# Expert weight conversion paced behind the dense layer's pieces, and half of g's low parts on GpSimd

## The chip, the cores and the metric

One core of one Trainium2 chip. The metric is the device time of one execution in microseconds (us), lower is better; each kernel is run several times.

## What is computed

Three layers follow each other (numpy, cut to what matters):

```python
def _attn_ref(q, k, v, g_norm):                  # q, k, v: 8 x 8 x 576 x 64
    kv = np.einsum('bhsd,bhse->bhde', k, v)
    out = np.einsum('bhsd,bhde->bhse', q, kv)
    rms = np.sqrt(np.mean(out * out, axis=-1, keepdims=True) + 1e-06)
    return out / rms * g_norm

def _moe_ref(x, w_in, w_out, alpha):             # x: 4608 x 512, w_in: 512 x 2048
    h = x @ w_in
    g = np.maximum(h, 0.0) + alpha * np.minimum(h, 0.0)
    return g @ w_out

def _moe2_ref(x, w_gate, w_output_gate, w1, w2): # 8 experts, w1[e]: 512 x 1024
    logits = x @ w_gate
    e_idx = np.argmax(logits, axis=1)
    ...
    for e in range(E):
        mask = e_idx == e
        out[mask] = gate_w[mask, None] * eom[mask, e, None] * (np.maximum(x[mask] @ w1[e], 0.0) @ w2[e])
```

## The kernel before, in words

Every float32 operand of a large product is split into two float16 halves, a high part and what is left (low part), and a product is three float16 matmuls: high by high, high by low, low by high. The 4608 tokens are 12 blocks of 384 (NBLK = 12), each of three tiles of 128.

The first 205 us are a stage whose order is written out by hand (`plan`, under `manual_schedule`): weights of the dense layer, attention for blocks 0 to 2, and the dense layer for blocks 0 and 1. Then come blocks 2 to 11, in which the order of each engine's queue is made by a list scheduler: it takes the instructions in the order in which the program writes them as their rank, and puts on each engine the first one that its own timing model holds to be ready. `tc.issue_after(ins)` adds the rule that what is written inside stands behind `ins` in the queue of the same engine. After block 11 come the expert slots, whose order on TensorE is again by hand.

A block i of 2 to 11 is written as `emit_h_block(i)`, then `emit_y_block(i)`.

- `emit_h_block` has 16 pieces f of h (128 of 2048 columns). A piece is 12 matmuls of 384 columns (`h_sum`, L689), ScalarE's scaled copy m out of PSUM (`h_copy`, L694), VectorE's maximum r (`h_bend`, L703), ScalarE's cast of r to the high part of g (`h_split`, L708) and VectorE's subtraction that makes the low part of g (L709). m and r have two buffers each, PSUM has two banks for h (`ps_h`). In the first stage GpSimd makes the low part (`start` is true), in blocks 2 to 11 VectorE does.
- `emit_y_block` has three row groups u of 128 tokens. Each is 48 matmuls of 512 columns (`y_products`, L724), three for each f, in two banks (`ps_y`). What is ready first goes first, so row groups of y are interleaved with pieces of h. The result is copied out (ysb, L736), scaled and split into rows (`y_tail`), turned by a transposing DMA, and goes to the logits (L802), the routing (`route_1`, `route_2`) and a scatter to DRAM by GpSimd (L868).
- After each piece, and after every fifth f of y, `tick` runs one item of each of several lists: `yq` (logits, routing), `side` (scatters), `attq` and, as often as it is told, `exq`.
- `attq` holds `att_steps(i)`, the attention for block i, 14 steps for i = 3 and on: q scaled on GpSimd (L328), split and transposed, products on TensorE (ops, L350), squares on ScalarE (L359), sums and scales on VectorE (L369 to L400), the power on GpSimd (L376), the cast (L411), the low part on GpSimd (L416) and the transposing DMA that makes x (L422). `att_steps(3)` runs in block 2's h pieces, `att_steps(i + 2)` from the y part of block i on.
- `exq` holds `expert_jobs`: 16 matrices of the experts (w1 and w2 of 8), each in four pieces of 128 x 1024. A piece is loaded (rawe, five buffers), its magnitude taken on ScalarE (eab, L624) and gathered on VectorE (L627). Then the maximum over partitions follows: a transpose on TensorE (allmax, L150), a row maximum on VectorE (L152), a matmul that spreads it (L154), in the one bank of `ps_l`, which logits and ranks use too. Then each piece is split into halves (ScalarE L475, VectorE L476) and stored to `ws`. Before, a matrix is 8 steps; `emit_h_block` runs a step at every third piece (6 per block), `emit_y_block` 9 per block. All of it must be done when block 10 ends.

Of the kernel before, what the change touches and what calls it, by code (L numbers as in the profile page):

```python
# [10 lines left out]
F32 = mybir.dt.float32  # L11
F16 = mybir.dt.float16
BF16 = mybir.dt.bfloat16
# [53 lines left out]
def body(ctx: ExitStack, tc, q, k, v, g_norm, w_in, w_out, alpha, w_gate, w_og, w1, w2, out):  # L67
# [76 lines left out]
            dve.tensor_scalar(out=out_s.bitcast(I32), in0=out_inv.bitcast(I32), scalar1=-1.0, scalar2=float(254 << 23),  # L144
                              op0=ALU.mult, op1=ALU.add)

    def all_max(am, nm):
        n = am.shape[1]
        ps = ps_l.tile([P, P + E], F32, tag="l", name="allmax" + nm)
        pe.transpose(ps[:n, 0:P], am, ident)  # L150
        m = small.tile([E, 1], F32, tag="amrow", name="amrow" + nm)
        dve.tensor_reduce(out=m[:n], in_=ps[:n, 0:P], axis=AX.X, op=ALU.max)  # L152
        if n == 1:
            pe.matmul(ps[:, P:P + 1], ones32[:1, :], m[:1], start=True, stop=True)  # L154
            return ps[:, P:P + 1]
        d = small.tile([E, E], F32, tag="amdiag", name="amdiag" + nm)
        dve.tensor_scalar(out=d[:n, :n], in0=ident[:n, :n], scalar1=m[:n], scalar2=None, op0=ALU.mult)
        pe.matmul(ps[:, P:P + n], ones32[:n, :], d[:n, :n], start=True, stop=True)
        return ps[:, P:P + n]
# [314 lines left out]
    def split(dst_h, dst_l, src, s):  # L474
        act.activation(out=dst_h, in_=src, func=AF.Copy, scale=s)  # L475
        dve.scalar_tensor_tensor(out=dst_l, in0=src, scalar=s, in1=dst_h, op0=ALU.mult, op1=ALU.subtract)  # L476

    def finish_max(am, nm):
        m = small.tile([P, 1], F32, tag="amx", name="amx" + nm)
        dve.tensor_reduce(out=m, in_=am, axis=AX.X, op=ALU.max)  # L480
        return all_max(m, nm)

    class Dense:

# [119 lines left out]
    def expert_jobs():  # L604
        raws = {}

        def load(n):
            if n < 8 * E:
                m, i = divmod(n, 4)
                src = (w1, w2)[m % 2][m // 2]  # L610
                r = src.shape[0] // 4
                t = rawp.tile([P, 1024], F32, tag="raw", name=f"rawe_{n}")
                sp.dma_start(out=t.rearrange("p (c f) -> p c f", f=src.shape[1]),
                             in_=src[i * r:(i + 1) * r, :].rearrange("(c p) f -> p c f", p=P))
                raws[n] = t

        for n in range(4):
            load(n)
        for m in range(2 * E):
            nm = f"_w{m}"  # L620
            am = cv.tile([P, 512], BF16, tag="acc", name="eam" + nm, bufs=1)
            for i in range(4):
                ab = cv.tile([P, 2, 512], BF16, tag="c", name=f"eab{nm}_{i}", bufs=3)
                act.activation(out=ab.rearrange("p a b -> p (a b)"), in_=raws[4 * m + i], func=AF.Abs)  # L624
                for h in range(2):
                    if i or h:
                        dve.tensor_tensor(out=am, in0=am if i else ab[:, 0, :], in1=ab[:, h, :], op=ALU.max)  # L627
                if i == 0:
                    load(4 * m + 4)
                yield  # L630
            for w in (256,):
                dve.tensor_tensor(out=am[:, 0:w], in0=am[:, 0:w], in1=am[:, w:2 * w], op=ALU.max)
            r = finish_max(am[:, 0:256], nm)
            s = small.tile([P, 1], F32, tag="es", name="es" + nm)
            inv = small.tile([P, 1], F32, tag=f"ei{m % 2}", name="ei" + nm)
            pow2(r, nm, s, inv)
            for i in range(4):
                w = ws[m // 2, :, m % 2 * 8192:(m % 2 + 1) * 8192].rearrange("p (t c) -> p t c", t=2)
                hi = stg.tile([P, 1024], F16, tag="hl", name=f"whi{nm}_{i}")
                lo = cv.tile([P, 1024], F16, tag="am", name=f"wlo{nm}_{i}")  # L640
                split(hi, lo, raws[4 * m + i], s)
                for t, (eng, x) in enumerate(((act, hi), (sp, lo))):
                    eng.dma_start(out=w[:, t, i * 1024:(i + 1) * 1024], in_=x)
                if i < 3:
                    load(4 * m + 5 + i)
                yield
            if m % 2 == 0:
                inv1 = inv
            else:
                dve.scalar_tensor_tensor(out=kexp[:, m // 2:m // 2 + 1], in0=inv1, scalar=1.0 / CB, in1=inv,  # L650
                                         op0=ALU.mult, op1=ALU.mult)


    attq, yq, exq, side = [], [], [], []

    def step(gens):
        while gens:
            if next(gens[0], "end") != "end":
                return
            gens.pop(0)  # L660
# [5 lines left out]
    def tick(n_expert=0):  # L666
        if yq:
            yq.pop(0)()
        if side:
            side.pop(0)()  # L670
        step(attq)
        for _ in range(n_expert):
            step(exq)


    def h_piece(i, f, g, start):
# [7 lines left out]
    def h_sum(i, f, ps):  # L684
        fs = slice(f % 4 * P, (f % 4 + 1) * P)
        n = 0
        for c in range(NC):
            for w, xc in ((0, c), (0, NC + c), (1, c)):
                pe.matmul(ps, wi[:, f // 4 * NC + c, w, fs], xt[i][:, xc, :], start=(n == 0), stop=(n == 3 * NC - 1))  # L689
                n += 1  # L690

    def h_copy(i, f, start, ps):
        r0 = tp.tile([P, BLK], F32, tag="m", name=f"m_{i}_{f}")
        act.activation(out=r0, in_=ps, func=AF.Copy, scale=(scst if start else scal)[:, f:f + 1])  # L694
        return i, r0

    def h_unit(f, g, start, part):
# [2 lines left out]
    def h_bend(f, part):  # L700
        i, r0 = part
        r = tp.tile([P, BLK], F32, tag="r", name=f"r_{i}_{f}")
        dve.scalar_tensor_tensor(out=r, in0=r0, scalar=alphat[:, f:f + 1], in1=r0, op0=ALU.mult, op1=ALU.max)  # L703
        return r

    def h_split(f, g, start, r):
        hi, lo = g[:, 0, f % GF, :], g[:, 1, f % GF, :]
        act.copy(out=hi, in_=r)  # L708
        (pool if start else dve).tensor_tensor(out=lo, in0=r, in1=hi, op=ALU.subtract)  # L709

    def emit_h_block(i):
        for f in range(NF):
            h_piece(i, f, gts[f // GF], False)
            if i == 2:
                for todo in (yq, side):
                    if todo:
                        todo.pop(0)()
            tick(f % 3 == 0)
        xt.pop(i)

    def y_products(ps, g, f, u, start, stop, **kw):
        us = slice(u * P, (u + 1) * P)
        for m, (t, w) in enumerate(((0, 0), (0, 1), (1, 0))):
            pe.matmul(ps, g[:, t, f % GF, us], wo[:, f, w, :], start=(start and m == 0), stop=(stop and m == 2), **kw)  # L724

    def emit_y_block(i):
        b = y_state(i)
        for u in range(TB):
            ps = ps_y.tile([P, DM], F32, tag="y", name=f"y_{i}_{u}")
            for f in range(NF):  # L730
                y_products(ps, gts[f // GF], f, u, f == 0, f == NF - 1)
                if f % 5 == 4:
                    tick(1)
            if i < NBLK - 1:
                ysb = cv.tile([P, DM], F32, tag="c", name=f"ysb_{i}_{u}", bufs=3)
                act.copy(out=ysb, in_=ps)  # L736
                ps = ysb
            y_tail(i, u, ps, *b)
        yq.append(lambda: route_1(i, *b))
# [43 lines left out]
    def row_turned(i, u, lg, rows, wait):  # L783
        nm = f"_{i}_{u}"
        rowt = rowts[u]
        row = rowt[:, 0:DM].bitcast(F16)
        rows.append(rowt)
        yT = tp.tile([P, 2 * NC, P], F16, tag="yT", name="yT" + nm, bufs=2)
        t = sp.dma_start_transpose(out=yT, in_=row)
        if (i, u) == (NBLK - 1, 0):  # L790
            sp_last[0] = t.ins
            rows_ahead()

        def logits():
            lps = ps_l.tile([P, 32], F32, tag="l", name="l" + nm)
            for c in range(NC):
                mm = [(yT[:, c, :], wg16[:, c].rearrange("p a b -> p (a b)"), lps),
                      (yT[:, NC + c, :], wg16[:, c, 0, :], lps[:, 0:16])]
                if c == NC - 1:
                    mm.reverse()  # L800
                for x, (a, w, o) in enumerate(mm):
                    pe.matmul(o, a, w, start=(c == 0 and x == 0), stop=(c == NC - 1 and x == 1))  # L802
            dve.tensor_reduce(out=lg[:, u, :], in_=lps.rearrange("p (t c) -> p c t", t=2), axis=AX.X, op=ALU.add)

        yq.extend([lambda: None] * wait + [logits])
# [720 lines left out]
```

## Time and profile before

| | us |
|---|---|
| median of three runs | 1359.05 |
| the three runs | 1351.5, 1359.05, 1364.7 |
| the profiled execution | 1348.63 |
| its span, first to last instruction | 1346.9 |
| mean granted TensorE clock | 0.983 |

The profile is of one execution. Engines are named PE (TensorE matmuls), PEld (TensorE weight loads), DVE (VectorE), ACT (ScalarE), POOL (GpSimd) and SP (the queue that issues most DMAs); PEq, ACTq, POOLq, SPq are their sequencers. Times in the trace are in us from the span's start. In square brackets stand the idle time of the engine ahead of a row and what ended it.

### The profile page before, as it was taken

Reading aid. Unit: us, or ns where it says so; the run is one execution under the profiler, and the core shown is the slowest. Engines: PE = TensorE matmul, PEld = TensorE weight load, DVE = VectorE, ACT = ScalarE, POOL = GpSimd, SP = SyncE. Lnnn points to the kernel's source line nnn. Section 1 sums busy time; section 2 is a strip of 40 time slices with the busy share of each in tenths; the row PEclk is TensorE's granted clock in tenths of the full one; section 3 lists DMA queues with packets and bytes.
Section 4 is the critical chain, followed back from the end, with each engine's and each line's share of the span. In section 5 each row is a group of like instructions: output and inputs, shape, how many; then the busy total and the mean of one; then the engine's idle time right before and its main releaser. Section 6 shows DMA issues by size and latency. Waiting matters only on the chain. (4 is left out here: it accounts for less than half of the span.)

```text
span 1346.9 us, 21979 instructions
## 1 busy us (share of the span) xinstructions
PE 1264.4 (94%) x7681; PEld 659.2 (49%) x7681; DVE 827.6 (61%) x2334; ACT 558.5 (41%) x928; POOL 334.4 (25%) x410
## 2 busy tenths in 40 slices
PE   5688999949989999999999999999999999999998
PEld 4444455525555554555555555554444444444443
DVE  7999876668778886969688787653712221222121
ACT  4455563436454655646555556440211111111111
POOL 4322221232222232223122222102232222222211
PEclk9799999979999999999999999999999999999999
DMA  9664127547595957775746665308999799799632
GB/s 308 155 172 124 57 71 190 125 150 187 150 235 142 251 164 195 197 209 133 229 97 189 173 181 149 108 12 308 180 264 246 152 326 264 138 250 266 129 86 55
DMA packets 322497, 236.22 MB, mean 175 GB/s; under 512 B 245436, under 2 KB 278220, under 8 KB 317904
## 3 DMA queue, kind: packets, MB, share of 16 engines
q1 hardware_dynamic: 303760, 189.05, 55.7%
q0 software_dynamic: 9216, 28.94, 6.5%
q10 hardware_dynamic: 9408, 16.79, 3.7%
q8 instruction: 62, 1.02, 0.3%
q14 instruction: 51, 0.42, 0.1%
HBM read 252.54 MB, written 53.25 MB: 227 GB/s over the span
## 5 line engine op out<-in xcount | busy, mean ns | idle before, releaser
L724 PE MATMUL y<-wo,g 128*128 128x512 f16 x1728 | 401.9, 381 | 7.7 <-DVE xs L400 5.8
L689 PE MATMUL h<-x,wi 128*128 128x384 f16 x1920 | 340.8, 329 | 22.1 <-DMA x<-x 17.2
L689 PEld LDWEIGHTS <-wi 128*128 128x128 f16 x2304 | 221.6, 98 | 180.5 <-issue 33.3
L724 PEld LDWEIGHTS <-g 128*128 128x128 f16 x1728 | 164.7, 98 | 192.6 <-issue 9.1
L1231 DVE CAST h_d<-br_d 128x512 f16<-128x512 f32 x62 | 26.9, 434 | 253.0 <-ACT br_d L1229 195.7
L708 ACT CAST g<-r 128x384 f16<-128x384 f32 x192 | 97.4, 509 | 129.0 <-DVE r L703 124.3
L703 DVE SCALAR_TENSOR_TENSOR r<-m,alphat 128x384 f32<-128x384 f32 x192 | 122.2, 639 | 17.9 <-ACT m L694 16.9
L1247 PEld LDWEIGHTS <-hT_d 128*128 128x128 f16 x744 | 72.4, 98 | 90.8 <-DMA hT_d<-h_d 2.6
L1225 PEld LDWEIGHTS <-byT_d 128*128 128x128 f16 x744 | 72.5, 98 | 88.2 <-issue 0.8
L376 POOL TENSOR_TENSOR rs<-ms,mhalf 128x8 f32<-128x8 f32 x36 | 66.3, 1846 | 183.2 <-DVE qm L382 136.8
L694 ACT ACTIVATE m<-h,scal 128x384 f32<-128x384 f32 x160 | 91.8, 574 | 33.5 <-PE h L689 32.1
L709 DVE TENSOR_TENSOR g<-r,g 128x384 f16<-128x384 f32 x160 | 91.7, 574 | 21.2 <-ACT g L708 20.2
L476 DVE SCALAR_TENSOR_TENSOR wlo_w<-rawe,es_w,whi_w 128x1024 f16<-128x1024 f32 x64 | 84.5, 1337 | 21.9 <-ACT whi_w L475 12.2
L1251 POOL DMA_INDIRECT out_dram<-ob_d,oidx_d x31 | 31.4, 1011 | 236.1 <-ACT ob_d L1250 219.9
L868 POOL DMA_INDIRECT ytab<-row,pos x36 | 38.8, 1077 | 203.9 <-DVE pos L849 112.0
L1229 ACT ACTIVATE br_d<-bh_d 128x512 f32<-128x512 f32 x62 | 37.0, 597 | 122.7 <-PE bh_d L1225 117.4
L624 ACT ACTIVATE eab_w<-rawe 128x1024 bf16<-128x1024 f32 x64 | 67.1, 1055 | 49.2 <-DMA rawe<-in_moe_w_dram 46.3
L475 ACT ACTIVATE whi_w<-rawe,es_w 128x1024 f16<-128x1024 f32 x64 | 70.9, 1142 | 28.5 <-DVE es_w L144 15.9
L1247 PE MATMUL bo_d<-lane,hT_d 128*128 128x512 f16 x360 | 80.2, 380 | 2.1 <-DMA hT_d<-h_d 2.1
L1225 PE MATMUL bh_d<-lane,byT_d 128*128 128x512 f16 x360 | 80.2, 379 | 0.0
L1250 ACT ACTIVATE ob_d<-bo_d,msc_d 128x512 f32<-128x512 f32 x31 | 21.3, 687 | 141.0 <-PE bo_d L1247 141.0
L689 PE MATMUL hbank<-x,wi 128*128 128x384 f16 x384 | 66.6, 331 | 6.3 <-DMA x<-x 4.5
(386 smaller groups left out, 1571.1 us busy)
## 6 DMA issues: line engine op xcount, KB each, us to landing
lane<-ws SPq DMA_DIRECT2D x74, 1024.0 KB
wi<-ws SPq DMA_DIRECT2D x44, 1024.0 KB
wo<-ws SPq DMA_DIRECT2D x36, 1024.0 KB
rawe<-in_moe_w_dram SPq DMA_DIRECT2D x64, 512.0 KB
ws<-whi_w ACTq DMA_DIRECT2D x64, 256.0 KB
ws<-wlo_w SPq DMA_DIRECT2D x64, 256.0 KB
rawwi<-in_moe_w_in_dram SPq DMA_DIRECT2D x16, 512.0 KB
rawwo<-in_moe_w_out_dram SPq DMA_DIRECT2D x16, 512.0 KB
```

Source lines behind the costliest of these rows:

```text
L376: pool.tensor_tensor(out=rs, in0=ms, in1=mhalf, op=ALU.pow)
L475: act.activation(out=dst_h, in_=src, func=AF.Copy, scale=s)
L476: dve.scalar_tensor_tensor(out=dst_l, in0=src, scalar=s, in1=dst_h, op0=ALU.mult, op1=ALU.subtract)
L624: act.activation(out=ab.rearrange("p a b -> p (a b)"), in_=raws[4 * m + i], func=AF.Abs)
L689: pe.matmul(ps, wi[:, f // 4 * NC + c, w, fs], xt[i][:, xc, :], start=(n == 0), stop=(n == 3 * NC - 1))
L694: act.activation(out=r0, in_=ps, func=AF.Copy, scale=(scst if start else scal)[:, f:f + 1])
L703: dve.scalar_tensor_tensor(out=r, in0=r0, scalar=alphat[:, f:f + 1], in1=r0, op0=ALU.mult, op1=ALU.max)
L708: act.copy(out=hi, in_=r)
L709: (pool if start else dve).tensor_tensor(out=lo, in0=r, in1=hi, op=ALU.subtract)
L724: pe.matmul(ps, g[:, t, f % GF, us], wo[:, f, w, :], start=(start and m == 0), stop=(stop and m == 2), **kw)
L1225: pe.matmul(hp[ts], j["yT"][:, x, ts], w1_[:, w, c, hs], start=(m == 0), stop=(m == 3 * NC - 1))
L1247: pe.matmul(po[ts], hT[:, g, ts], w2_[:, w, f, :], start=(m == 0), stop=(m == 3 * NFE - 1))
```

## The change

It has five parts. (1) `expert_jobs` is cut into `magnitude`, `scale` and `halves`: the transpose, the row maximum and the spreading matmul of `scale` stand one step apart, the next matrix's first magnitude is taken between them, five pieces are loaded ahead instead of four, and a matrix is 9 steps (145 in all). (2) `scale` uses a bank of `ps_y` while h pieces are written and one of `ps_h` while y is written, instead of `ps_l`. (3) `tick` runs at most one expert step and puts its instructions behind the last h or y instruction written so far on PE, ACT and DVE (`paced`); a step is written at every second piece of h instead of every third. The logits' matmuls are put behind the last product on PE. (4) In block 2 `attq` is stepped twice per piece. (5) In blocks 2 to 11 GpSimd makes the low part of g for odd f.

```diff
+        def scale(m):
...
+            dve.tensor_reduce(out=col, in_=am[:, 0:256], axis=AX.X, op=ALU.max)
+            yield
+            pool_, tag = idle[0]
+            ps = pool_.tile([P, P + E], F32, tag=tag, name="allmax" + nm)
+            pe.transpose(ps[:1, 0:P], col, ident)
+            row = small.tile([E, 1], F32, tag="amrow", name="amrow" + nm)
+            dve.tensor_reduce(out=row[:1], in_=ps[:1, 0:P], axis=AX.X, op=ALU.max)
+            yield
+            pe.matmul(ps[:, P:P + 1], ones32[:1, :], row[:1], start=True, stop=True)
...
+        def halves(m, i):
...
+            split(hi, lo, raws[4 * m + i], scs[m][0])
+            for t, (eng, x) in enumerate(((act, hi), (sp, lo))):
+                eng.dma_start(out=w[:, t, i * 1024:(i + 1) * 1024], in_=x)
+            load(4 * m + 5 + i)
+
+        for n in range(5):
+            load(n)
+        magnitude(0, 0)
+        yield
+        for m in range(2 * E):
+            for i in range(1, 3):
+                magnitude(m, i)
+                yield
+            magnitude(m, 3)
+            steps = scale(m)
+            next(steps)
+            yield
+            if m + 1 < 2 * E:
+                magnitude(m + 1, 0)
+            next(steps)
+            yield
+            next(steps, None)
+            yield
             for i in range(4):
...
+                halves(m, i)
                 yield
...
         step(attq)
-        for _ in range(n_expert):
-            step(exq)
+        if n_expert and exq:
+            with ExitStack() as behind_h:
+                for ins in paced.values():
+                    behind_h.enter_context(tc.issue_after(ins))
+                step(exq)
...
+        paced["pe"] = t.ins
...
+        paced["act"] = t.ins
...
+        paced["dve"] = t.ins
...
-        (pool if start else dve).tensor_tensor(out=lo, in0=r, in1=hi, op=ALU.subtract)
+        (pool if start or f % 2 else dve).tensor_tensor(out=lo, in0=r, in1=hi, op=ALU.subtract)
 
     def emit_h_block(i):
+        idle[0] = ps_y, "y"
         for f in range(NF):
             h_piece(i, f, gts[f // GF], False)
             if i == 2:
                 for todo in (yq, side):
                     if todo:
                         todo.pop(0)()
-            tick(f % 3 == 0)
+                step(attq)
+            tick(f % 2 == 0)
...
     def emit_y_block(i):
         b = y_state(i)
+        idle[0] = ps_h, "h"
...
-                    pe.matmul(o, a, w, start=(c == 0 and x == 0), stop=(c == NC - 1 and x == 1))
+                    with tc.issue_after(paced["pe"]):
+                        pe.matmul(o, a, w, start=(c == 0 and x == 0), stop=(c == NC - 1 and x == 1))
```

## Rows read from the trace of the kernel before

**Rows 1.** The page, part 1: busy us (share of the span) and instructions.
```profile
PE 1264.4 (94%) x7681; PEld 659.2 (49%) x7681; DVE 827.6 (61%) x2334; ACT 558.5 (41%) x928; POOL 334.4 (25%) x410
```
**Rows 2.** Windows by stage: length, busy of each engine, granted clock, DMA, GB/s.
```profile
core 0: us, PE busy (x) PEld busy (x) DVE busy (x) ACT busy (x) POOL busy (x), PEclk, DMA share, GB/s
205.00:283.60 78.60, 75.32 (x587) 42.72 (x584) 50.74 (x173) 26.14 (x54) 15.25 (x15) 1.00 0.55 127
283.60:300.40 16.80, 0.03 (x1) 0.05 (x1) 13.13 (x37) 8.34 (x9) 10.15 (x9) 0.53 0.82 267
300.40:307.40 7.00, 6.94 (x36) 3.72 (x36) 1.50 (x4) 2.31 (x4) 0.74 (x1) 0.67 0.98 281
307.40:945.00 637.60, 620.03 (x3986) 335.20 (x3984) 484.94 (x1426) 339.42 (x551) 154.44 (x141) 1.00 0.63 173
945.00:1346.90 401.90, 392.38 (x1974) 178.19 (x1972) 99.06 (x264) 71.20 (x115) 92.15 (x145) 1.00 0.80 197
```
**Rows 3.** Timeline: the longest wait of PE, and the chain ahead of it.
```profile
206.69 6.01 PE L689 MATMUL h<-x,wi 128*128 128x384 f16 x36 [0.38 <-DMA x<-x]
...
254.87 0.83 PE L350 MATMUL ops<-kv,qT 128*128 128x128 f16 x12
...
268.74 0.58 ACT L736 COPY ysb<-y 128x512 f32<-128x512 f32 x1 [2.38 <-PE y L724]
...
272.82 0.58 ACT L359 ACTIVATE xs<-ops 128x512 f32<-128x512 f32 x1
...
287.98 2.13 DVE L476 SCALAR_TENSOR_TENSOR wlo_w<-rawe,es_w,whi_w 128x1024 f16<-128x1024 f32 x1
290.04 0.68 DVE L400 TENSOR_TENSOR xs<-ops,rs 128x512 f32<-128x512 f32 x1
...
296.21 2.22 SPq L422 DMA_TRANSPOSE x<-x  x1
...
300.46 6.14 PE L689 MATMUL h<-x,wi 128*128 128x384 f16 x23 [16.84 <-DMA x<-x]
```
**Rows 4.** PE's waits, 301 to 945 us: in total, times, longest.
```profile
PE ops L350 <- DMA qT<-q: 5.8, 4, 2.6
PE h L689 <- ACT m L694: 4.8, 4, 1.9
PE l L802 <- DMA yT<-row: 4.2, 3, 2.5
PE allmax_w L150 <- DVE lg L803: 1.4, 1, 1.4
PE allmax_w L150 <- DVE xinv L389: 0.6, 1, 0.6
PE y L724 <- DVE g L709: 0.6, 1, 0.6
```
**Rows 5.** Timeline of ACT and PE around two waits of h for m.
```profile
413.52 1.06 ACT L624 ACTIVATE eab_w<-rawe 128x1024 bf16<-128x1024 f32 x1 [1.76 <-DMA rawe<-in_moe_w_dram]
...
415.58 2.11 PE L689 MATMUL h<-x,wi 128*128 128x384 f16 x12 [1.90 <-ACT m L694]
...
485.73 1.06 ACT L624 ACTIVATE eab_w<-rawe 128x1024 bf16<-128x1024 f32 x1 [4.56 <-DMA rawe<-in_moe_w_dram]
...
488.24 4.06 PE L689 MATMUL h<-x,wi 128*128 128x384 f16 x24 [1.77 <-ACT m L694]
```
**Rows 6.** Lines 709 and 416: durations in ns (least/median/most), first and last start.
```profile
L709 DVE TENSOR_TENSOR g<-r,g x160: 534/553/1512, 210.7 to 912.2; 128x384 f16<-128x384 f32 x160
L709 POOL TENSOR_TENSOR g<-r,g x32: 907/948/1717, 56.2 to 193.9; 128x384 f16<-128x384 f32 x32
...
L416 POOL TENSOR_TENSOR x<-xs,x x27: 1146/1162/5593, 246.8 to 843.9; 128x512 f16<-128x512 f32 x27
```
**Rows 7.** Timeline: a DVE subtraction beside a GpSimd multiplication.
```profile
411.77 1.04 POOL L286 TENSOR_TENSOR kvsc<-kvbd,kvs 128x512 f32<-128x512 f32 x1 [10.37 <-DVE qsc L144]
...
411.78 1.45 DVE L709 TENSOR_TENSOR g<-r,g 128x384 f16<-128x384 f32 x1
```
**Rows 8.** GpSimd's groups of instructions, 300.4 to 945 us: busy us, mean ns.
```profile
L416 POOL TENSOR_TENSOR x<-xs,x 128x512 f16<-128x512 f32 x24 | 35.9, 1494 | 83.0 <-ACT x L411 64.4 <-issue 12.6 <-DVE g L709 6.0
```

More of the change, by code (lines that the diff above doesn't have):

```diff
@@ L145, in pow2, with all_max @@
                               op0=ALU.mult, op1=ALU.add)
-    def all_max(am, nm):
+    def all_max(am, nm, pool_=None, tag="l"):
         n = am.shape[1]
-        ps = ps_l.tile([P, P + E], F32, tag="l", name="allmax" + nm)
+        ps = (pool_ or ps_l).tile([P, P + E], F32, tag=tag, name="allmax" + nm)
         pe.transpose(ps[:n, 0:P], am, ident)
@@ L476, in split, with finish_max @@
         dve.scalar_tensor_tensor(out=dst_l, in0=src, scalar=s, in1=dst_h, op0=ALU.mult, op1=ALU.subtract)
-    def finish_max(am, nm):
+    def finish_max(am, nm, *bank):
         m = small.tile([P, 1], F32, tag="amx", name="amx" + nm)
         dve.tensor_reduce(out=m, in_=am, axis=AX.X, op=ALU.max)
-        return all_max(m, nm)
+        return all_max(m, nm, *bank)
     class Dense:
@@ L615, in load, with magnitude @@
                 raws[n] = t
-        for n in range(4):
-            load(n)
-        for m in range(2 * E):
+        sums, scs = {}, {}
+        def magnitude(m, i):
             nm = f"_w{m}"
[L621 to L633, printed above, removed]
+            if i == 0:
+                sums[m] = cv.tile([P, 512], BF16, tag="acc", name="eam" + nm, bufs=1)
+            am = sums[m]
+            ab = cv.tile([P, 2, 512], BF16, tag="c", name=f"eab{nm}_{i}", bufs=3)
+            act.activation(out=ab.rearrange("p a b -> p (a b)"), in_=raws[4 * m + i], func=AF.Abs)
+            for h in range(2):
+                if i or h:
+                    dve.tensor_tensor(out=am, in0=am if i else ab[:, 0, :], in1=ab[:, h, :], op=ALU.max)
@@ new lines, in scale @@
+        def scale(m):
+            nm = f"_w{m}"
+            am = sums.pop(m)
+            dve.tensor_tensor(out=am[:, 0:256], in0=am[:, 0:256], in1=am[:, 256:512], op=ALU.max)
+            col = small.tile([P, 1], F32, tag="amx", name="amx" + nm)
+            dve.tensor_reduce(out=col, in_=am[:, 0:256], axis=AX.X, op=ALU.max)
[7 more added lines that the diff above has]
+            pe.matmul(ps[:, P:P + 1], ones32[:1, :], row[:1], start=True, stop=True)
@@ L634, in expert_jobs @@
             s = small.tile([P, 1], F32, tag="es", name="es" + nm)
             inv = small.tile([P, 1], F32, tag=f"ei{m % 2}", name="ei" + nm)
-            pow2(r, nm, s, inv)
-            for i in range(4):
[L638 to L645, printed above, removed]
-                yield
@@ L647, in expert_jobs @@
[L647 to L651, printed above, removed]
+            pow2(ps[:, P:P + 1], nm, s, inv)
+            scs[m] = s, inv
+            if m % 2:
+                dve.scalar_tensor_tensor(out=kexp[:, m // 2:m // 2 + 1], in0=scs[m - 1][1], scalar=1.0 / CB, in1=inv,
+                                         op0=ALU.mult, op1=ALU.mult)
@@ new lines, in halves @@
+        def halves(m, i):
+            nm = f"_w{m}"
+            w = ws[m // 2, :, m % 2 * 8192:(m % 2 + 1) * 8192].rearrange("p (t c) -> p t c", t=2)
+            hi = stg.tile([P, 1024], F16, tag="hl", name=f"whi{nm}_{i}")
+            lo = cv.tile([P, 1024], F16, tag="am", name=f"wlo{nm}_{i}")
+            split(hi, lo, raws[4 * m + i], scs[m][0])
+            for t, (eng, x) in enumerate(((act, hi), (sp, lo))):
+                eng.dma_start(out=w[:, t, i * 1024:(i + 1) * 1024], in_=x)
+            load(4 * m + 5 + i)
@@ L654, in body @@
     attq, yq, exq, side = [], [], [], []
+    paced, idle = {}, [None]
     def step(gens):
@@ L688, in h_sum @@
             for w, xc in ((0, c), (0, NC + c), (1, c)):
-                pe.matmul(ps, wi[:, f // 4 * NC + c, w, fs], xt[i][:, xc, :], start=(n == 0), stop=(n == 3 * NC - 1))
+                t = pe.matmul(ps, wi[:, f // 4 * NC + c, w, fs], xt[i][:, xc, :], start=(n == 0), stop=(n == 3 * NC - 1))
                 n += 1
+        paced["pe"] = t.ins
     def h_copy(i, f, start, ps):
         r0 = tp.tile([P, BLK], F32, tag="m", name=f"m_{i}_{f}")
-        act.activation(out=r0, in_=ps, func=AF.Copy, scale=(scst if start else scal)[:, f:f + 1])
+        t = act.activation(out=r0, in_=ps, func=AF.Copy, scale=(scst if start else scal)[:, f:f + 1])
+        paced["act"] = t.ins
         return i, r0
@@ L702, in h_bend @@
         r = tp.tile([P, BLK], F32, tag="r", name=f"r_{i}_{f}")
-        dve.scalar_tensor_tensor(out=r, in0=r0, scalar=alphat[:, f:f + 1], in1=r0, op0=ALU.mult, op1=ALU.max)
+        t = dve.scalar_tensor_tensor(out=r, in0=r0, scalar=alphat[:, f:f + 1], in1=r0, op0=ALU.mult, op1=ALU.max)
+        paced["dve"] = t.ins
         return r
@@ L723, in y_products @@
         for m, (t, w) in enumerate(((0, 0), (0, 1), (1, 0))):
-            pe.matmul(ps, g[:, t, f % GF, us], wo[:, f, w, :], start=(start and m == 0), stop=(stop and m == 2), **kw)
+            t = pe.matmul(ps, g[:, t, f % GF, us], wo[:, f, w, :], start=(start and m == 0), stop=(stop and m == 2), **kw)
+        paced["pe"] = t.ins
     def emit_y_block(i):
         b = y_state(i)
+        idle[0] = ps_h, "h"
         for u in range(TB):
@@ L735, in emit_y_block @@
                 ysb = cv.tile([P, DM], F32, tag="c", name=f"ysb_{i}_{u}", bufs=3)
-                act.copy(out=ysb, in_=ps)
+                paced["act"] = act.copy(out=ysb, in_=ps).ins
                 ps = ysb
```

## The prediction

> **What bounds the kernel now.** I read the page's first part, then the windows by stage, then what TensorE (PE) waits for, then the timeline around its longest wait. PE is busy for 94% of the span [rows 1]; every other engine is far from that (VectorE, DVE, 61%). The windows [rows 2] say where the other 6% lie in the stretch that the change touches: 205 us (block 2 starts) to 945 us (block 11 ends). PE is idle for 78.6 - 75.3 = 3.3 us in block 2, for all of 283.6 to 300.4, and for 637.6 - 620.0 = 17.6 us from 307.4 to 945. After 945 the expert slots keep PE at 392.4 of 401.9 us; the change does not reach them. So PE sets the time, and the change can gain only where PE waits or runs slowly.
>
> The reader is to see one wait in rows 3: PE idles 16.84 us at 300.46 until x, block 3's input, has been turned. Block 2's last matmul lies right before, so no other matmul stands in the queue ahead. Followed back: the third tile's products leave PE at 254.87, but ScalarE (ACT) squares them only at 272.82, its queue having waited for the row copy ysb (268.74) and the routing's exponentials; on DVE an expert piece (wlo, 2.13 us) stands in front of xs (290.04); the cast, the low part on GpSimd (POOL) and the transpose (296.21) follow. It is an order of queues, not a lack of engine time: DVE is busy for 50.7 of block 2's 78.6 us [rows 2]. During the wait the granted clock falls to 0.53 and is 0.67 in the next 7 us [rows 2], that is for part of the time at 1.2 GHz instead of 2.4.
>
> **Attention twice per piece in block 2.** att_steps(3) has 14 steps, the last making that third tile. At one step per piece it is written behind piece 13 (counted from 0), at two behind piece 6. Block 2's pieces take about (254.87 - 206.69)/16 = 3.0 us each [rows 3], so the tile's work stands 7 x 3.0 = 21 us earlier in program order, more than the 16.84 us wanted, and its square (ready near 235 instead of 256) no longer stands behind the ysb of 268.74. I take the whole wait as gone: -16.8 us. The clock's share goes with it: 23 h matmuls took 6.14 us after the wait [rows 3] and 24 take 4.06 us at full clock [rows 5], so 6.14 - 4.06 x 23/24 = 2.2 us. Sum -19.0. Ends: 0 (another link of the chain is late just as long) and -19.0. Late next would be block 3's h pieces themselves, at ACT and DVE.
>
> **Expert conversion.** Its work stays the same in ACT and DVE operations; 128 steps become 16 x 9 + 1 = 145, and the ticks per block go from 6 + 9 = 15 to 8 + 9 = 17. 128/15 and 145/17 are both 8.53 blocks, so it ends in block 10 as before. What changes is place. Each step's PE, ACT and DVE instructions are now queued behind the last h or y instruction written so far. That meets two kinds of wait among the 17.4 us of rows 4. First, 4.8 us of h waiting for ACT's copy m: in the pairs of rows 5 ACT stood idle on an expert piece whose load had not landed (1.76 us before 413.52, 4.56 us before 485.73), with the copy behind it, and PE then waited 1.90 and 1.77 us. Second, the maximum over partitions took the only bank of ps_l, shared with logits and ranks: 1.4 us of allmax waiting for the sum lg, which frees it, and 0.6 us for DVE's queue. It now has an idle bank, and its two matmuls stand one tick apart, which moves DVE's part out from between them. The logits' matmuls, queued behind the products, meet the 4.2 us of l waiting for yT. Addressed: 4.8 + 2.0 + 4.2 = 11.0 us. Not addressed: 5.8 us of ops waiting for qT. Loads are not put behind anything, but the lead from a load to its use is 4 steps now and was 5, so waits for raw pieces will not vanish. I take 8 of the 11 as gained: -8.0. Ends: +5 (the 4.8 us of waits for m double, as the shorter lead allows) and -11.
>
> **GpSimd makes every second low part.** 8 pieces in each of 10 blocks, 80 subtractions, leave DVE. There the median is 553 ns; GpSimd's for the same shape in the first stage is 948 ns [rows 6]. DVE gets 80 x 0.553 = 44 us back, POOL gets 80 x 0.948 = 76 us on top of 154 in 638 us, which fits. Neither is the bound: DVE has 637.6 - 484.9 = 153 us idle there [rows 2], so what it gets back is worth little by itself. What it costs is delay, 948 - 553 = 0.4 us per odd piece before y may use it, and contention. The contention is seen in [rows 7]: a DVE subtraction that starts 0.01 us after a GpSimd multiplication lasts 1.45 us instead of 0.55. The other way about, GpSimd's subtractions of x have a median of 1.162 us but a longest of 5.593 us [rows 6]. By the Trainium skill (page "SBUF — State Buffer", section "Who interferes with whom") a DVE instruction with two SBUF inputs and a GpSimd instruction that reads SBUF exclude each other, and whichever starts second waits for the whole of the first; these rows agree. It speaks against the change, since the released DVE time is partly paid back. Even if every one of the 80 cost DVE 1.45 - 0.55 = 0.90 us, that is 72 - 44 = 28 us more of DVE in 153 us of idle time.
>
> For PE the bounds are: below, -3, as a shorter DVE queue could shorten half of the 5.8 us for qT; above, every odd low part late for y, by the 0.4 us plus the 0.33 us by which the mean of GpSimd's subtractions stands over their median (1.494 [rows 8] and 1.162 us [rows 6]): 80 x 0.73 = +58 us. Now y waits for g for 0.6 us in all [rows 4], so the order leaves room nearly everywhere, and I take the value near that end: one in eight late, 80/8 = 10 of them, each by 0.5 of the 0.73 us: +5.
>
> **Sum.** -19.0 - 8.0 + 5.0 = -22.0 us. On the profiled execution (1348.63 us, span 1346.9) that is 1326.6. The three runs have the median 1359.05, 10.4 us above it; -22 us on the median gives the forecast, 1337 us, 1.6% faster. The runs shown differ by 13 us, so about 1% is what a measurement of this kernel can tell from no change.
>
> **Rivals.**
> (a) The wait before block 3 is only traded. For it: the chain runs over five queues, and two attention steps per piece, two routings and the expert steps now meet in block 2. Against it: the 21 us of advance. Half of 19.0 stays and the ACT and logit waits stay: -9.5 + 5 = -4.5, 1354.5 us.
> (b) Slower: the low parts on GpSimd hold up y. Place: y's first row group, which PE runs interleaved with h and which uses each g soon after it is made. Price +58, with -19.0 and -8.0 kept: +31, 1390 us. Also each r buffer (two of them) stays held until GpSimd has read it. It decides when nearly half of the odd pieces come late ((19 + 8)/0.73 = 37 of 80). For it: the 5.593 us of rows 6. Against it: the 0.6 us of rows 4, and a program order that was made with the slower engine in it. The Trainium skill's page "SBUF — State Buffer" (section "Who interferes with whom") names the same lock.
> (c) Nearly all PE waits from 205 to 945 go: -16.8 - 2.2 - 17.4 = -36.4, 1322.7 us. For it: most waits have a named queue order as cause. Against it: qT's 5.8 us are untouched.
> (d) The GpSimd part does nothing measurable, since DVE is not the bound: this is inside the forecast, at -27 instead of -22 (1332).
>
> **How the numbers follow.** Forecast with (d) 0.58, (a) 0.20, (b) 0.13, (c) 0.09. Under 1345.5 us (1% faster) lie (c) and most of the forecast (0.54): 0.63. Within 1%: 0.04 of the forecast, all but 0.01 of (a): 0.23. Slower: (b) and 0.01: 0.14. The range reaches from a little below (c) to halfway into (b): 1317 to 1367 us; the forecast's own range is 1326 to 1348.
>
> **What would show it.** Right: no PE gap above 3 us between blocks 2 and 3, the clock at 1.00 there, the third square within a few us of its products, fewer waits of h for m and of l for yT, and block 11 ending near 920 instead of 945. GpSimd's 80 low parts at 0.9 to 1.3 us, y waiting for GpSimd's g for under 6 us in all. Wrong: y or r waiting for GpSimd in every block; a new wait at the first h of block 3; ACT idle on raw pieces in front of h's copies; or a PE clock below 1 in a stretch that had it.

## The result, and the profile after

The changed kernel takes 1346.3 us (median of 12 runs, 1337.9 to 1356.0), the kernel before 1359.4 (12 runs): ratio 0.9911, 95% interval 0.9882 to 0.9939. It is 0.9% faster, 13 us, where 22 us (1337 us) were forecast; the range held, and most of the forecast's largest term did not come.

Its first profiled execution took 1344.09 us, span 1342.4. Part 1 of its page, beside [rows 1]:

```profile
PE 1266.6 (94%) x7681; PEld 660.2 (49%) x7681; DVE 822.5 (61%) x2254; ACT 559.2 (42%) x928; POOL 406.9 (30%) x490
```

The 80 moved subtractions are there (DVE 2254 instructions instead of 2334, POOL 490 instead of 410). POOL gained 72.5 us of work. DVE lost 5.1, and not the 44 us of the subtractions that left it.

The windows below stand at events of the changed kernel: block 2's h pieces, the rest of block 2's y, block 3, blocks 4 to 11, the expert slots (columns as in [rows 2]).

```profile
207.10:257.40 50.30, 46.08 (x390) 28.20 (x391) 39.54 (x132) 23.54 (x42) 16.76 (x15) 1.00 0.65 158
257.40:296.70 39.30, 32.68 (x194) 16.04 (x193) 30.05 (x104) 18.94 (x29) 15.33 (x15) 0.87 0.75 194
296.70:376.00 79.30, 72.67 (x467) 38.90 (x465) 59.87 (x164) 43.45 (x68) 29.34 (x29) 0.96 0.73 196
376.00:936.00 560.00, 548.34 (x3514) 297.59 (x3513) 415.85 (x1158) 293.20 (x478) 191.00 (x187) 1.00 0.61 169
936.00:1342.40 406.40, 396.36 (x1992) 180.10 (x1990) 101.33 (x271) 72.59 (x117) 92.70 (x145) 1.00 0.82 197
```

The same five stretches of the kernel before, at its own events:

```profile
206.70:257.50 50.80, 49.61 (x419) 30.23 (x420) 37.24 (x124) 19.75 (x39) 12.73 (x11) 1.00 0.68 167
257.50:281.30 23.80, 23.42 (x131) 10.86 (x130) 9.92 (x35) 5.06 (x11) 1.53 (x4) 1.00 0.26 57
281.30:380.40 99.10, 75.33 (x491) 40.91 (x489) 75.07 (x218) 52.07 (x79) 29.48 (x27) 0.90 0.70 191
380.40:941.00 560.60, 548.64 (x3525) 296.92 (x3523) 423.75 (x1248) 297.33 (x484) 136.83 (x126) 1.00 0.62 173
941.00:1346.90 405.90, 396.38 (x1992) 179.95 (x1990) 101.70 (x271) 72.48 (x117) 92.15 (x145) 1.00 0.80 197
```

The third row fell by 19.8 us: the wait before block 3 is gone. The second row grew by 15.5 us: the end of block 2's y takes 39.3 us instead of 23.8. Together blocks 2 and 3 gained 173.7 - 168.9 = 4.8 us; the other rows hardly moved in this pair. The two spans differ by 4.5 us only, where the medians differ by 13: the first profile of the kernel before is of an execution 10.8 us below its median. PE's timeline after block 2's last h shows what fills the 39.3 us (beside the last row of [rows 3]):

```profile
258.14 0.83 PE L350 MATMUL ops<-kv,qT 128*128 128x128 f16 x12
258.81 9.88 PE L764 MATMUL y<-wo,g 128*128 128x512 f16 x45
270.60 1.04 PE L764 MATMUL y<-wo,g 128*128 128x512 f16 x4 [1.91 <-ACT g L746]
274.97 0.39 PE L845 MATMUL l<-wg,yT 128*128 128x32 f16 x8 [3.33 <-DMA yT<-row]
276.13 1.46 PE L350 MATMUL ops<-kv,qT 128*128 128x128 f16 x12 [0.77 <-DMA qT<-q]
277.39 2.77 PE L764 MATMUL y<-wo,g 128*128 128x512 f16 x6
...
296.77 1.46 PE L724 MATMUL h<-x,wi 128*128 128x384 f16 x8
```

The chain behind the third tile's products, on ACT and on SP's queue:

```profile
260.77 0.58 ACT L359 ACTIVATE xs<-ops 128x512 f32<-128x512 f32 x1
...
268.81 1.24 SPq L422 DMA_TRANSPOSE x<-x  x1
```

Block 3's h starts at 296.77 instead of 300.46. Its input was there 27 us earlier (the last transpose of x is issued at 268.81, before at 296.21), but PE still had 119 of block 2's 144 y matmuls to do when block 2's last h was over; before, it had 102. Three waits make 6.0 us, and the clock is low there too: the stretch's mean is 0.87, so 12 products that take 0.83 us at 258.14 take 1.46 at 276.13.

PE's waits from 205 to 943 us in the changed kernel, beside [rows 4]:

```profile
PE ops L350 <- DMA qT<-q: 7.7, 7, 1.9
PE h L724 <- ACT m L730: 6.7, 8, 2.3
PE y L764 <- POOL g L747: 4.2, 3, 2.7
PE l L845 <- DMA yT<-row: 3.3, 1, 3.3
PE y L764 <- ACT g L746: 1.9, 1, 1.9
```

Of the kinds that the prediction wanted to shrink, h for m stands at 6.7 us against 4.8 and l for yT at 3.3 against 4.2. In the second profiles of the two kernels it is 5.5 against 6.4 and 3.7 against 4.4, so neither total moved by more than two executions differ.

### The profile page after: what moved, and what is told of

Same layout as the page of the kernel before. It is cut to its first block, busy times and chain, and to the rows that moved or that the text cites. A ratio compares the mean times of both kernels' runs of the same rounds, so it can differ in the third digit from the quotient of the medians.

```text
span 1342.4 us, 22084 instructions
## 1 busy us (share of the span) xinstructions
PE 1266.6 (94%) x7681; PEld 660.2 (49%) x7681; DVE 822.5 (61%) x2254; ACT 559.2 (42%) x928; POOL 406.9 (30%) x490
## 4 chain that ended last, share of the span: by engine, by line
PE 56%; DVE 7%; DMA 5%; issue 4%; POOL 1%; ACT 1%; SPq 0%; POOLq 0%; DVEq 0%; ACTq 0%
PE y L764 14%; PE bo_d L1290 12%; PE h L724 12%; PE bh_d L1268 11%; PE bo_s L1290 2%; DMA rawe<-in_moe_w_dram 1%; PE bh_s L1268 1%; DVE r L740 1%; PE bo_p L1290 1%; PE bh_p L1268 1%; DMA q<-in_q_dram 1%; DMA qT<-q 1%; DMA hT_d<-h_d 1%; PE kvps L263 1%; PE ops L350 1%
## 5 line engine op out<-in xcount | busy, mean ns | idle before, releaser
L764 PE MATMUL y<-wo,g 128*128 128x512 f16 x1728 | 396.6, 383 | 13.3 <-DVE xs L400 5.8
L724 PE MATMUL h<-x,wi 128*128 128x384 f16 x1920 | 334.7, 328 | 7.2 <-ACT m L730 6.7
L764 PEld LDWEIGHTS <-g 128*128 128x128 f16 x1728 | 166.9, 99 | 207.9 <-issue 13.3
L747 POOL TENSOR_TENSOR g<-r,g 128x384 f16<-128x384 f32 x112 | 112.4, 1005 | 317.9 <-ACT g L746 245.0
L740 DVE SCALAR_TENSOR_TENSOR r<-m,alphat 128x384 f32<-128x384 f32 x192 | 131.5, 687 | 39.5 <-ACT m L730 37.5
L911 POOL DMA_INDIRECT ytab<-row,pos x36 | 41.7, 1158 | 71.9 <-DMA ytab<-row,pos 38.2
```

The costliest lines, as they stand in the source:

```text
L724: t = pe.matmul(ps, wi[:, f // 4 * NC + c, w, fs], xt[i][:, xc, :], start=(n == 0), stop=(n == 3 * NC - 1))
L740: t = dve.scalar_tensor_tensor(out=r, in0=r0, scalar=alphat[:, f:f + 1], in1=r0, op0=ALU.mult, op1=ALU.max)
L747: (pool if start or f % 2 else dve).tensor_tensor(out=lo, in0=r, in1=hi, op=ALU.subtract)
L764: t = pe.matmul(ps, g[:, t, f % GF, us], wo[:, f, w, :], start=(start and m == 0), stop=(stop and m == 2), **kw)
```

## The experiments

Each was built from one of the two kernels. "Blocks 2+3" runs from the first h of block 2 to the last y of block 3, "blocks 4-11" on to the last y of block 11, "slots" to the end; they are counted in each profile's timeline, one execution each, in us (a y counts from its start). In brackets behind the median stands the time of the execution that was profiled: e9's is the slowest of its runs, 9.5 us above the median, and those of e3, e8 (first) and e11 are the quickest of theirs. The ratio is to the kernel before, measured along with it, with its 95% interval.

| kernel | median (profiled) | ratio | blocks 2+3 | blocks 4-11 | slots |
|---|---|---|---|---|---|
| before (two profiles) | 1359.4 (1348.6, 1359.6) | 1 | 173.6, 174.1 | 560.7, 562.8 | 405.9, 410.4 |
| changed (two profiles) | 1346.3 (1344.1, 1345.5) | 0.9911 (0.9882 to 0.9939) | 168.9, 170.4 | 560.0, 557.5 | 406.4, 405.7 |
| e1: changed, no GpSimd part | 1349.0 (1348.1) | 0.9936 (0.9917 to 0.9955) | 163.5 | 564.0 | 411.0 |
| e2: changed, attention once | 1352.3 (1348.6) | 0.9962 (0.9936 to 0.9988) | 172.9 | 559.5 | 405.9 |
| e9: changed, neither | 1353.3 (1362.9) | 0.9964 (0.9940 to 0.9989) | 168.0 | 566.7 | 418.2 |
| e3: before + GpSimd part | 1374.8 (1367.9) | 1.0127 (1.0092 to 1.0161) | 175.9 | 569.0 | 412.9 |
| e4: before + attention twice | 1364.6 (1365.7) | 1.0050 (1.0025 to 1.0075) | 161.2 | 578.7 | 413.6 |
| e5: changed, rule on place out | 1362.3 (1362.9) | 1.0028 (0.9997 to 1.0058) | 172.3 | 570.1 | 408.2 |
| e8: changed, bank of attention | 1345.4 (1337.5) | 0.9914 (0.9886 to 0.9941) | 163.2 | 558.1 | 406.3 |
| e8 once more | 1342.3 (1342.0) | 0.9878 (0.9852 to 0.9904) | 164.6 | 559.1 | 406.1 |
| e10: e8, no GpSimd part | 1355.9 (1356.2) | 0.9972 (0.9948 to 0.9997) | 162.8 | 564.7 | 418.6 |
| e11: changed, f = 15 on VectorE | 1349.6 (1345.3) | 0.9932 (0.9907 to 0.9956) | 166.9 | 562.2 | 405.6 |

**Both kernels once more.** These two set the scale: what does one profile say?

> The kernel before once more, for a second profile: how far stages differ from execution to execution. If the stages repeat, the middle (first h of block 2 to last y of block 11) is within 2 us of 734.3 us with the 16.8 us wait in it, and the rest of the 10 us between the profiled execution and the median lies in the first stage or the expert slots.

> The changed kernel once more, for a second profile. If the stages repeat, the middle is within 2 us of 728.9 us and block 2 takes 88 to 91 us.

Measured: the kernel before 1359.6 us, the changed one 1345.5, each close to its median. The stages repeat within about 3 us: middle 736.9 (2.6 above the first profile, where 2 were expected) and 727.9, block 2 of the changed kernel 90.3 us. The first profile of the kernel before was a quick execution: the second has 3.8 us more in the first stage (210.5 against 206.7), 2.6 in the middle and 4.5 in the slots. The second pair differs by 14.1 us, as the medians do: 9.0 in the middle, 4.7 in the slots, 0.4 ahead of block 2. A difference of a few us between two rows of the table is no finding by itself.

**e2, attention stepped once.** In `emit_h_block` of the changed kernel:

```diff
-                step(attq)
             tick(f % 2 == 0)
```

> The changed kernel with attention stepped once per piece in block 2. Theory A (the double step is what took the 16.8 us wait away): the wait of h for x before block 3 is back with 10 us or more, time 1352 to 1362 us. Rival B (the expert instructions behind the pieces took it away, since they no longer stand in front of the third tile's square and scale): no wait over 4 us there, time 1346 +- 4.

Measured: 1352.3 us, the lower end of theory A's range. The wait of h for x is not back, as rival B has it, but the input is late again:

```profile
261.05 0.83 PE L350 MATMUL ops<-kv,qT 128*128 128x128 f16 x12
...
274.89 0.58 ACT L359 ACTIVATE xs<-ops 128x512 f32<-128x512 f32 x1
...
292.94 1.23 SPq L422 DMA_TRANSPOSE x<-x  x1
...
298.68 0.81 PE L763 MATMUL y<-wo,g 128*128 128x512 f16 x3
299.33 0.33 PE L724 MATMUL h<-x,wi 128*128 128x384 f16 x1
```

The square stands 13.8 us behind its products, and x is turned at 292.94, not far from the kernel before (296.21). PE does not wait for it, because block 2's y, which starts right behind the expert maximum (see e8), ends at 299.5 instead of 281.5; blocks 2 and 3 take 172.9 us, against 173.6 and 174.1. With the second step they are 2.5 to 4 us shorter (168.9 and 170.4 in the changed kernel), and 4.5 without the GpSimd part (e1 163.5, e9 168.0). The profiles divide by it. With the double step (changed, e1, e4, e5, e8, e10, e11) the square comes 1.1 to 3.3 us behind its products and the last transpose of x at 269 to 276 us; without it (before, e2, e3, e9) 13.8 to 18.0 us behind and at 293 to 299. So the double step is what makes x early. The expert part alone does not (e9); with it block 2's y is late enough to fill the wait.

**e4, attention stepped twice, alone.** The same line added to the kernel before:

```diff
+                step(attq)
             tick(f % 3 == 0)
```

> The kernel before with only the second attention step per piece in block 2 added. Theory A (this alone makes block 3's input early): the 16.8 us wait gone, about 1342 us, ratio 0.987. Rival B (block 2 gets longer by what the wait gets shorter, as y no longer runs between its pieces): block 3's first h less than 6 us earlier, ratio 0.993 to 1.0.

Measured: 1364.6 us, slower. The wait is gone and block 3's first h comes 26 us earlier (274.2), so both theories fall: blocks 2 and 3 gain 12 us, and then blocks 4 to 11 lose 16 to 18. Its waits of PE (205 to 955 us) say where:

```profile
PE h L689 <- ACT m L694: 10.1, 8, 2.9
PE y L725 <- ACT ysb L737: 9.9, 4, 3.5
```

Both wait for ACT copies. ACT's own waits in e4 (first row), the kernel before, the changed kernel and e5 (last row) go with it; each row is from one kernel's waits of ACT, blocks 2 to 11:

```profile
ACT eab_w L624 <- DMA rawe<-in_moe_w_dram: 52.5, 32, 3.9
```
```profile
ACT eab_w L624 <- DMA rawe<-in_moe_w_dram: 45.5, 25, 4.6
```
```profile
ACT eab_w L625 <- DMA rawe<-in_moe_w_dram: 18.7, 14, 2.9
```
```profile
ACT eab_w L625 <- DMA rawe<-in_moe_w_dram: 25.0, 20, 3.0
```

While ACT waits for an expert's load, the copies of h and y queued behind it wait too [rows 5]. Of e4's 20.0 us of PE waiting for m and ysb, 10.7 have such a wait of ACT in the 4 us ahead of them or within them. The wait before block 3 was time in which the expert pieces caught up: when block 3's last y starts, ACT has begun 15 magnitudes and 12 high parts of pieces in the kernel before, 13 and 8 in e4. What is left over stands in the way later.

**e5, the rule on place taken out.**

```diff
             with ExitStack() as behind_h:
-                for ins in paced.values():
-                    behind_h.enter_context(tc.issue_after(ins))
                 step(exq)
```

> The changed kernel without the rule that expert instructions stand behind the last h or y instruction (the logits' rule stays). Theory G (pacing is what keeps waiting expert pieces out of the way of ACT's copies; the double step alone ran into 10 us of h waiting for m and 10 us of y waiting for ysb): 10 us or more of waits more, 1356 us or more. Rival H (the new steps and banks do it, not the rule): 1346 +- 4.

Measured: 1362.3 us, theory G. One waiting pattern replaces another; PE's waits in e5:

```profile
PE h L722 <- ACT m L728: 15.0, 13, 2.5
PE ops L350 <- DMA qT<-q: 9.2, 5, 2.7
PE y L762 <- ACT g L744: 9.2, 2, 8.6
```

Of e5's 15.0 us of h waiting for m, 9.4 have a wait of ACT for a raw piece in the 4 us ahead of them or within them; in the kernel before it is 4.5 of 4.8, in the changed kernel 0.4 of 6.7 (second profiles: 5.9 of 6.4 and 0.4 of 5.5). So the rule does keep waiting pieces out of the way of the copies. What h waits for in the changed kernel is something else: ahead of its longest wait (2.3 us, to 477.99) ACT's cast of g had waited for DVE's r.

Of all parts tried one by one, this costs most to leave out: 16 us.

**e3 and e1, the GpSimd part alone, and all but it.** e3 has the new subtraction line in the kernel before, e1 the old line in the changed one:

```diff
-        (pool if start else dve).tensor_tensor(out=lo, in0=r, in1=hi, op=ALU.subtract)
+        (pool if start or f % 2 else dve).tensor_tensor(out=lo, in0=r, in1=hi, op=ALU.subtract)
```

> The kernel before with only the GpSimd part added. Theory A (5 us cost): about 1364 us, ratio 1.004, the 16.8 us wait still there. Rival B (VectorE's relief helps the chain of block 3's input, which an expert piece on VectorE held up): the wait shorter by 5 us or more and the time 1350 or less.

> The changed kernel with every low part of g in blocks 2 to 11 back on VectorE. Theory A (the prediction's step: the GpSimd part costs about 5 us, as y waits for it and VectorE is held up): about 1341 us, 0.987 of the kernel before, y waiting for GpSimd's g 0 instead of 4.2 us. Rival B (VectorE's relief is what lets the pieces of h keep pace): slower than the changed kernel's 1346, 1351 us or more. Rival C (it does nothing): 1346 +- 4.

Measured: e3 1374.8 us, 1.3% slower, more than theory A; the long wait is still there, now as products waiting for q:

```profile
301.51 1.46 PE L350 MATMUL ops<-kv,qT 128*128 128x128 f16 x12 [16.45 <-DMA qT<-q]
```

e1 takes 1349.0 us. Theory A's 0.987 lies outside its interval; its interval and the changed kernel's overlap, so rivals B and C are not told apart by the time. DVE's load is told, by part 1 of the pages of e3 (beside [rows 1]) and of e1 (beside the changed kernel's above):

```profile
PE 1276.9 (93%) x7681; PEld 663.0 (49%) x7681; DVE 827.0 (61%) x2254; ACT 557.7 (41%) x928; POOL 408.0 (30%) x490
```
```profile
PE 1268.8 (94%) x7681; PEld 661.6 (49%) x7681; DVE 833.0 (62%) x2334; ACT 558.6 (41%) x928; POOL 328.8 (24%) x410
```

The 44 us of subtractions leave DVE, and its busy time falls by 0.6 us (827.6 to 827.0; 2.2 against the second profile of the kernel before) in one pair and by 10.5 us (833.0 to 822.5) in the other. The rest is paid back as longer DVE instructions; the mean of r goes from 639 ns, in the row of the kernel before, to 684 in e3's:

```profile
L703 DVE SCALAR_TENSOR_TENSOR r<-m,alphat 128x384 f32<-128x384 f32 x192 | 122.2, 639 | 17.9 <-ACT m L694 16.9
```
```profile
L703 DVE SCALAR_TENSOR_TENSOR r<-m,alphat 128x384 f32<-128x384 f32 x192 | 131.0, 684 | 27.3 <-ACT m L694 23.9 <-POOL g L709 1.6 <-POOL row L865 0.7
```

The trace shows which ones: in e3, 62 of the 192 r run beside a two-input operation of GpSimd (TENSOR_TENSOR) and take 840 ns in the mean, the other 130 take 610; in the kernel before 40 run beside one, at 747 ns, and the other 152 take 611. That is the contention of [rows 7]; its size here is 34 to 44 us for 80 operations, 0.4 to 0.55 us each. The Trainium skill states the rule in "SBUF — State Buffer", section "Who interferes with whom": a DVE instruction with two SBUF inputs contends with a GpSimd instruction that reads SBUF. These rows agree.

Why e3 is slower by 17 us is not settled: its profile has 6 to 8 us more in blocks 4 to 11, and PE's busy time is 10 to 12 us above the two profiles of the kernel before, with the mean clock at 0.977 instead of 0.983 and 0.982.

**e11, the last low part of a block back on VectorE.** The changed kernel has y waiting for GpSimd's g in three places. The longest, in block 3, first PE and then POOL:

```profile
353.72 2.73 PE L764 MATMUL y<-wo,g 128*128 128x512 f16 x6 [2.67 <-POOL g L747]
```
```profile
351.64 0.97 POOL L911 DMA_INDIRECT ytab<-row,pos  x1 [6.68 <-issue]
352.60 0.20 POOL L908 COPY row<-ids 128x1 int32<-128x1 int32 x1
352.75 0.92 POOL L747 TENSOR_TENSOR g<-r,g 128x384 f16<-128x384 f32 x1
```

The low part stands behind a scatter ahead of which GpSimd was idle for 6.68 us.

```diff
-        (pool if start or f % 2 else dve).tensor_tensor(
+        (pool if start or f % 2 and f < NF - 1 else dve).tensor_tensor(
```

> The changed kernel with the last piece of each block (f = 15) back on VectorE, 70 instead of 80 low parts on GpSimd. Theory K (y waited for GpSimd in 3 or 4 places, 4.2 and 6.4 us in two profiles, mostly at a block's last low part queued behind a scatter that waited): y's wait for GpSimd's g under 1.5 us, time 3 to 5 us less, 1341 to 1343. Rival C (another wait takes its place): 1346 +- 3.

Measured: y's wait for GpSimd is down to 1.4 us in one place, as theory K has it; h's wait for m is 10.2 us instead of 6.7, and the time is 1349.6, not theory K's 1341 to 1343 and just above rival C's 1343 to 1349.

**e8, where the expert maximum has its bank.** The changed kernel's timeline shows block 2's and block 3's first y right behind the expert maximum's transpose:

```profile
234.63 0.27 PE L639 MATMUL allmax_w<-ident,amx_w 128*1 128x128 f32 x1 [1.09 <-DVE amx_w L635]
234.74 1.02 PE L764 MATMUL y<-wo,g 128*128 128x512 f16 x4
...
329.70 0.27 PE L639 MATMUL allmax_w<-ident,amx_w 128*1 128x128 f32 x1
329.81 1.46 PE L764 MATMUL y<-wo,g 128*128 128x512 f16 x6
```

Before, the first y comes 6 us after block 2's first h; here 28. The bank of y that the maximum takes while h is written was the suspect:

```diff
-            pool_, tag = idle[0]
+            pool_, tag = ps_a, "a"
```

> The changed kernel with the expert maximum in one of the three banks of attention (ps_a), instead of a bank of y while h is written and a bank of h while y is written. Theory D (in blocks 2 to 5 the first row group of y stands in the same pool behind the expert maximum and starts only 0.1 us after its transpose, so y no longer runs between the pieces of h; this gave back what the wait before block 3 had brought): block 2's first y about 6 us after its first h instead of 28, 40 or more of its 144 y matmuls ahead of its last h instead of 25, block 2's first h to last y 80 us or less instead of 89, time 1332 to 1340 us. Rival E (block 2 got longer because attention, two routings and expert steps meet there, and not because of the bank): y early but block 2 still 86 us or more, time 1346 +- 4. Rival F (the attention bank becomes the wait): ops waiting longer, 1350 us or more.

> The kernel with the attention bank once more. Its profile had a middle of 721.3 us, 7 us under the changed kernel's 728.9 and 727.9, but its median 1345.4 us was no better than 1346.3. If the 7 us are real, the middle is again under 724 us and the median 1337 to 1342; if that execution was a quick one, the middle is 726 to 730 and the median 1345 +- 3.

Measured: 1345.4 and 1342.3 us. The mechanism is as theory D has it: the first y of block 2 comes 5.8 us after its first h (timeline of the second run below), 48 of its y matmuls lie ahead of its last h, where the changed kernel has 25.

```profile
210.40 6.01 PE L724 MATMUL h<-x,wi 128*128 128x384 f16 x36 [0.47 <-DMA x<-x]
216.25 1.03 PE L764 MATMUL y<-wo,g 128*128 128x512 f16 x4
```

Theory D's time (1332 to 1340 us) and its 80 us or less for block 2 did not come: block 2 takes 95 us, and by these two measures rival E fits. Block 2's length says little here, though, as block 3's h now starts at 275.0, before block 2's y ends. Blocks 2 and 3 together are 163.2 and 164.6 us, 4 to 7 less than in the changed kernel, and the middle is 721.3 and 723.7 against 728.9 and 727.9. The medians are 1 and 4 us lower, and the intervals overlap; the second run is at the edge of what was expected if the gain is real (under 724 us, 1337 to 1342). In e5 the first y is early too (5.9 us after the first h), as without the rule the maximum itself comes early, at 214.39. So the bank, together with the rule that makes the maximum late, explains why y stood late; that e8 is faster than the changed kernel is likely by its profiles and not shown by the times.

**e9 and e10, two more combinations.** e9 is the changed kernel with the edits of e1 and e2 together; e10 is e8 with the edit of e1.

> The changed kernel without the GpSimd part and without the double attention step: the new expert steps, their banks and the rule on their place alone. Theory I (this part is what makes the others harmless and pays by itself): 0.994 to 0.998 of the kernel before, 1350 to 1355 us. Rival J (the parts only work together): 1358 us or more. First y of block 2 right behind the expert maximum, as in the changed kernel.

> The expert maximum in a bank of attention, and every low part of g in blocks 2 to 11 on VectorE. Theory C (the GpSimd part does nothing for the time, as VectorE is not the bound and the lock gives back most of what it saves): equal to the kernel with the attention bank, 1345 +- 4. Theory A (GpSimd's low parts cost about 5 us): 1340. Rival B (they help): 1350 or more. VectorE's busy time 10 us or less above that of the kernel with the attention bank, although 44 us of subtractions come back.

Measured: e9 1353.3 us, theory I: the expert part is the one part that pays by itself (0.4%). e10 1355.9 us, rival B: without GpSimd's low parts the kernel with the attention bank is slower by 10 us and more, and the intervals are apart. Its DVE is busy for 831.8 us, e8's for 826.8 and 828.9. Of the 14 to 19 us between its profile and e8's, 12 lie in the slots (418.6 against 406.3 and 406.1), though nothing in them was edited, and 4 to 6 in the middle. In e10's slots PE waits 10.6 us for loads (hT_d and yT), in e8's 3.0 and 2.5. All six profiles that have both the expert part with its rule and low parts on GpSimd (the changed kernel twice, e2, e8 twice, e11) show 405.6 to 406.4 there; the three with the expert part and VectorE alone show 411.0 to 418.6. But the kernel before, without either, shows 405.9 and 410.4 in two executions, its waits for these loads being 2.9 and 5.8 us. What makes the loads late, and whether GpSimd's low parts have to do with it, is not shown.

Two parts were not tried by themselves: the new order of the expert work in nine steps per matrix, and the rule that puts the logits' matmuls behind the products.

## Why the prediction was right or wrong

**PE sets the time, and the change gains only where PE waits: right in the middle.** PE's idle time there falls from 37.3 to 29.1 us in the first pair of profiles and from 38.6 to 28.7 in the second, the middle by 5.4 and 9.0. So 4 to 8 of the 13 us between the medians lie elsewhere: in the second pair 4.7 are in the slots, which the change was held not to reach, and no run shows why.

**"I take the whole wait as gone: -16.8 us" and "Sum -19.0": the term that failed.** The wait did go, x came 27 us earlier, and the third square came 2.6 us after its products (260.77 against 258.14) instead of 18. That much of the mechanism was right, and it is the double step's doing (e2). But blocks 2 and 3 gained 4.7 us in the first pair of profiles and 3.7 in the second. Three things in the step were wrong:

- It said that the tile's work moves by 7 pieces, its square "ready near 235". The products left at 258.14, before at 254.87. The scheduler did not move them with the program; what got better was the order on ACT and DVE behind them.
- It took the end of the wait for a gain of the same size. In e2 the wait is gone though x is late, since the late y of block 2 fills it, and blocks 2 and 3 gain 1 us; the second step is worth 2.5 to 4 us there, by the changed kernel and e2, and 4.5 by e1 and e9, and not 19; in e4 it is gone and x is early, and blocks 4 to 11 lose more than was gained.
- "Late next would be block 3's h pieces themselves" was wrong. Late next was block 2's own y. The new bank put its first row group behind the expert maximum (shown by e8), and PE is idle for 10.8 us in block 2, where it had been for 1.6: it waits for the logits' yT (3.3), attention's loads of v (2.1), casts of g (1.9), qT (1.8) and the expert maximum (1.1).

**"I take 8 of the 11 as gained: -8.0": not as written.** h for m and l for yT were 9.0 us and are 10.0 (second profiles: 10.8 and 9.2). The cause that was named did go: waits of h for m with ACT idle on a raw piece fell from 4.5 us to 0.4. Other waits for m, behind DVE's r among them, came in their place, so the total stayed; it was a term priced as if nothing stood behind it. The rule's worth is rather in what it keeps from coming: without it (e5) h waits for m 15.0 us and all is 16 us slower. ACT's 45.5 us of waiting for raw loads, of which the prediction names the two pairs of [rows 5], leave room for that.

**"+5" for GpSimd: right in the wait, wrong in the frame.** y waited for GpSimd's g 4.2 us (6.4 in the second profile) where +5 and "under 6" stood. That VectorE gets only part of its 44 us back was said, too; it got 0.6 to 10.5 us. But taking the part out does not bring 5 us back (e1), alone it costs 17 us (e3), and with the attention bank the kernel that has it is quicker by at least 10 (e10). So its price is not fixed; it differs with the order around it, and why is not shown. That it does nothing measurable in the changed kernel (rival (d)) is not excluded by e1.

**The sum** was 9 us too good. Parts were priced one by one and added. Measured one by one they are +1.3%, +0.5% and -0.4%, which add to +1.4%; together they are -0.9%. Rival (a), the wait only traded, came closest for blocks 2 and 3; its 1354.5 us was 8 us too high. Rivals (b) and (c) did not occur. Of the signs that the prediction named, the early square, low parts near 0.9 us and the small wait for GpSimd (4.2 us, but 6.4 in the second profile) came. The clock at 1.00 between blocks 2 and 3 and the end of block 11 near 920 did not (936.4), and a sign of being wrong did: the rest of block 2 had a clock of 1.00 and has 0.87.

## What to carry to other kernels

A wait that is gone is not yet time gained: look whether its cause went or other work of the engine slid into its place (e2). A long wait of the bounding engine is also time in which the other engines catch up: before pricing its removal, count what they did during it and where that work will stand afterwards (e4). When a scheduler makes the order, price a set of edits as a set and test the parts in both directions, alone and left out. A buffer borrowed from a pool in the middle of the program can hold back the pool's next user, as the bank of y did here (e8).

## What the runs showed of the hardware that was not expected

Moving 44 us of two-input subtractions from VectorE to GpSimd freed little on VectorE: 0.6 to 10.5 us. Blocks 2 to 11 of one and the same kernel repeat within 3 us, but in the kernel before the first stage (206.7 and 210.5) and the expert slots (405.9 and 410.4) differ by about 4 us each between two executions, as much as some of the single edits here are worth.
